# One first-layer matmul per step, issued in two, three or four column pieces

## The chip, the cores and the metric

The kernel runs on one core of a Trainium2 chip. The metric is the device time of one launch in microseconds; lower is better. A profile of one execution gives, beside that time, the span from the first to the last instruction of the program and every instruction's start and length.

## What is computed

Two stages follow one another. The first is a spectral mixer on `x` of shape (8, 3008, 256); the second a two-layer network on its 24064 rows.

```python
X = rfft(x, axis=1)                       # 8 batches, length 3008 along the rows
Yr = Xr @ w_r - Xi @ w_i + b_r
Yi = Xr @ w_i + Xi @ w_r + b_i
Y  = sign(Y) * max(abs(Y) - 0.01, 0)      # real and imaginary part
y  = irfft(Y, n=3008, axis=1)
h  = y.reshape(24064, 256) @ w_in         # 256 -> 2048
g  = where(h > 0, h, exp(min(h, 0)) - 1)
out = g @ w_out                           # 2048 -> 256
```

## The kernel before, in words

**The main loop (L1050).** The network is cut into 47 blocks of 512 rows, and each block into 8 pairs of 128 of the 2048 hidden columns: 376 steps, one pair of one block each. A step has a first layer and a second layer.

- First layer: `front_mm(i, h, 0)` and `front_mm(i, h, 1)` (L836, matmuls at L841). Each fills one tile `hps` of 128 hidden columns by 512 rows with two bf16 matmuls, `dt` 0 and 1, for the two halves of the 256 input columns. Where a block of 512 rows lies across the edge of two batches, `pieces` (L823) gives two stretches of rows, and each is a matmul of its own; that is so in 7 of the 47 blocks, so in 56 steps.
- The activation: ScalarE (L855, L856 or L858), GpSimd (L863) and VectorE (L875) turn `hps` into `gT`, in fp32r (a 4-byte form that TensorE takes).
- Second layer: `back(i - 2)` (L879, matmuls at L893), two steps behind: 8 matmuls, each with a 128 x 128 piece of `gT` as weights and 256 columns of `w_out_r` streamed, into `ps_o`. "The group" below is these 8.

**The units.** The mixer of the next batches is cut into units that run inside the steps, at most one per step, issued between `front_mm(i, h, 0)` and `front_mm(i, h, 1)`:

- A (L145): two fp32r matmuls of 512 columns;
- X (L188): eight bf16 matmuls of 96 columns;
- M (L250): six bf16 matmuls of 256 columns;
- B (L331): four bf16 matmuls of 256 columns (for batch 1, eight of half height);
- Y (L389): eight bf16 matmuls of 94 columns.

`units()` (L945) gives each unit its step ahead of time, from due times of the batches, and `plan()` (L1011) puts it into `f0[i]`. Of the 376 steps 84 have an M, 62 a Y, 56 an X, 42 a B, 36 an A and 96 have no unit. The order on TensorE is the order of issue:

```python
front_mm(i, h, 0)
for f, a in f0[i]:
    f(*a)                 # the unit, if there is one
front_mm(i, h, 1)
...
back(i - LAG)             # LAG = 2
```

Nothing reorders it. What TensorE can wait for is a free `hps` (4 buffers, two steps' worth, given back by L875), a `gT` that is ready (L875), and the data of the unit. Every matmul goes with a load of its 128 x 128 weights (the row PEld of the profile), also where the same weights are there already.

Of the kernel before, what the change touches and what calls it, by code (L numbers as in the profile page):

```python
# [25 lines left out]
def kernel(  # L26
# [11 lines left out]
    nc = tc.nc  # L38
    P = nc.NUM_PARTITIONS
# [20 lines left out]
    w_in_s = constp.tile([P, 2, DFF], BF16, name="w_in_s")  # L60
# [31 lines left out]
    TB = 512  # L92
# [17 lines left out]
    yT_of = {}  # L110
# [316 lines left out]
    with tc.tile_pool(name="stagep", bufs=1) as stagep:  # L427
# [3 lines left out]
        def col(eng, src, s1, op0, s2=None, op1=None, n=1, dt=F32):  # L431
            t = stagep.tile([P, n], dt, name=f"c{len(cols)}")
            cols.append(t)
            if op1 is None:
                eng.tensor_scalar(t[:], src[:], s1, None, op0)
            else:
                eng.tensor_scalar(t[:], src[:], s1, s2, op0, op1)
            return t

        def mix(eng, a, sc, b, op0, op1, n=1):  # L440
            t = stagep.tile([P, n], F32, name=f"c{len(cols)}")
            cols.append(t)
            eng.scalar_tensor_tensor(t[:], a[:], sc, b[:], op0, op1)
            return t
# [72 lines left out]
        c1 = mix(dve, qcol, -2.0, pcol, ALU.mult, ALU.add)  # L517
        c0 = col(dve, c1, -1.0, ALU.mult, 1.0, ALU.add)
# [304 lines left out]
    def pieces(t, k):  # L823

        out_, c = [], 0
        while c < k:
            b, r = divmod(t + c, S)
            e = min(k, c + S - r)
            out_.append((b, r, c, e))
            c = e  # L830
        return out_

    def front_ps():
        return [psH.tile([P, TB], F32, name="hps", tag="hps")[:] for _ in range(2)]

    def front_mm(i, hps, s):  # L836
        blk, fp = divmod(i, NPAIR)
        ft = 2 * fp + s
        for b, t0, c0, c1 in sorted(pieces(blk * TB, TB), key=lambda z: z[3] - z[2]):
            for dt in range(2):  # L840
                nc.tensor.matmul(  # L841
                    hps[s][:, c0:c1], lhsT=w_in_s[:, dt, ft * P : ft * P + P],
                    rhs=yT_of[b][:, dt, t0 : t0 + c1 - c0],
                    start=(dt == 0), stop=(dt == 1),
                )

    class Elu:
        def __init__(self, i, hps, mode):
# [162 lines left out]
    def plan():  # L1011

        f0 = [[] for _ in range(n + PER)]
        f1 = [[] for _ in range(n + PER)]
        mid = [[] for _ in range(n + PER)]
        at, xat = units()
        for (kind, b, k), t in at.items():
            if kind == "M" and k < 11 and (
                k % 2 == 0 if b == 1 else at[kind, b, k + 1] == t + 1
            ):  # L1020
                whole.add((b, k))
        for (kind, b, k), t in at.items():
            if t == 0:
                continue
            name = "Y" if kind == "y" else kind
            f0[t].append(put(name, b, *((k // 2, k % 2) if kind == "M" else (k,))))
            if (kind, k) == ("X", 7):
                for j in range(2):
                    mid[t + 1 + j].append((unit_D, (b, j)))
            if (kind, k) == ("B", 5):  # L1030
                f1[t + (b > 1)] += [(load_Bs, (b, w)) for w in range(4)]
            if (kind, k) == ("A", 5):
                for p in range(2 if b == 2 else 4):
                    w = 8 if p == 0 or b > 2 else 24
                    f1[t + (0, 1, 3)[min(max(b - 2, 0), 2)] * p].append((load_Z, (b, 8 * p, 8 * p + w)))
        for (b, c), t in xat.items():
            f1[t].append((load_x, (b, c)))
        for k in range(3):
            f1[5 + k].append((weight_sum, (k,)))
        for c in range(2):  # L1040
            f1[24 + c].append((turn_M3, (c,)))
            f1[4 + c].append((scale_w_in, (3, True, slice(FQ // 2 * c, FQ // 2 * c + FQ // 2))))
        return f0, f1, mid

    NST = 2
    f0, f1, mid = plan()
# [3 lines left out]
    for i in range(n + LAG):  # L1050
        split = False
        if i < n:
# [3 lines left out]
            h = front_ps()  # L1056
            e = Elu(i, h, "dve" if i < 4 else {"M": "act", "F": "pool"}[kind])
            front_mm(i, h, 0)
            for f, a in f0[i]:
                f(*a)  # L1060
            front_mm(i, h, 1)
            if was:
                was.mix(1 if kind == "M" and len(was.todo) == 2 else 0 if kind == "M" else 2)
# [69 lines left out]
```

## Time and profile before

| what | value |
|---|---|
| time, median of 3 runs | 884.24 us (883.89 to 884.44) |
| time of the profiled execution | 884.42 us |
| its span, first to last instruction | 882.4 us |
| granted TensorE clock, mean | 1.000 |
| TensorE matmul busy | 866.6 us, 6745 matmuls |
| second-layer matmuls (L893) | 3008 recorded, 478.9 us |
| first-layer matmuls (L841) | 1728 recorded, 438.3 us |
| ScalarE, VectorE, GpSimd busy | 726.7, 658.4 and 653.3 us |

The time of a run is some 2 us more than the span, which leaves out what lies around the program. A matmul's recorded length (382 ns for 512 columns at L841) is more than the distance from its start to the next one's, so successive matmuls overlap in the record: what one costs is that distance. The trace gives these starts to the nanosecond.

### The profile page before, as it was taken

To read this page: it belongs to the slowest core of one execution; us is meant where nothing else is said; L and a number is where in the kernel's file an instruction comes from. 1 tells how busy PE (TensorE), PEld (TensorE's weight loads), DVE (VectorE), ACT (ScalarE), POOL (GpSimd) and SP (SyncE) were. 2 spreads that over 40 slices of the span, in tenths; PEclk is the share of its full clock that TensorE was granted. 3 is DMA by queue.
4 is the path that set the end of the run, shared out by engine and by line. 5 is a ranking of instruction groups with operands and counts; after the bars stand their busy time and mean duration, and the time that the engine had idled before them with its cause. 6 is when DMAs were issued, how large, how long until landed. Compare 5 with 4: busy or idle time off the path is not lost.

```text
span 882.4 us, 18403 instructions
## 1 busy us (share of the span) xinstructions
PE 866.6 (98%) x6745; PEld 672.0 (76%) x6745; DVE 658.4 (75%) x1066; ACT 726.7 (82%) x1217; POOL 653.3 (74%) x981
## 2 busy tenths in 40 slices
PE   8889999999999999999999999999999999999997
PEld 3447777877788777878779777787777877787775
DVE  8767886688777787677876777767776688777775
ACT  6668998899878998899978999789987888786664
POOL 6707995689767887698866888668886699756664
PEclk9999999999999999999999999999999999999999
DMA  8994346743485443643464444553444023431111
GB/s 263 348 266 132 94 121 186 194 145 94 120 247 160 118 122 107 173 143 94 132 177 138 129 123 118 156 168 91 134 119 136 25 67 83 119 88 32 43 31 49
DMA packets 106374, 116.55 MB, mean 132 GB/s; under 512 B 10886, under 2 KB 96012, under 8 KB 103404
## 3 DMA queue, kind: packets, MB, share of 16 engines
q1 hardware_dynamic: 100124, 87.85, 35.8%
q0 software_dynamic: 6016, 27.40, 10.0%
q8 instruction: 53, 0.87, 0.4%
q14 instruction: 37, 0.30, 0.1%
q10 hardware_dynamic: 144, 0.13, 0.0%
HBM read 55.32 MB, written 49.81 MB: 119 GB/s over the span
## 4 chain that ended last, share of the span: by engine, by line
PE 86%; POOL 5%; DVE 5%; DMA 2%; issue 1%; ACT 1%; SPq 0%; POOLq 0%; DVEq 0%
PE ps_o L893 36%; PE hps L841 34%; PE mps L262 5%; PE xps L197 2%; PE aps L163 2%; PE yps L397 2%; POOL Et L863 2%; PE bps L356 1%; PE mps L214 1%; POOL Y L293 1%; DVE gT L875 1%; DMA w_in_f<-in_moe_w_in_dram 1%; PE bps L347 1%; DMA xt<-in_x_dram 1%; DVE yb L279 1%
## 5 line engine op out<-in xcount | busy, mean ns | idle before, releaser
L875 DVE SCALAR_TENSOR_TENSOR gT<-Et,hps 128x512 fp32r<-128x512 f32 x752 | 493.5, 684 | 161.6 <-POOL Et L863 160.3
L893 PE MATMUL ps_o<-w_out_r,gT 128*128 128x256 f32 x3008 | 478.9, 301 | 0.1
L863 POOL TENSOR_SCALAR Et<-Et 128x512 f32<-128x512 f32 x576 | 351.5, 618 | 166.5 <-ACT Et L858 165.3
L893 PEld LDWEIGHTS ps_o<-w_out_r,gT 128*128 128x128 f32 x3008 | 403.9, 188 | 49.7 <-DVE gT L875 0.3
L841 PE MATMUL hps<-yT,w_in_s 128*128 128x512 bf16 (+4 forms) x1728 | 438.3, 354 | 2.6 <-DVE gT L875 1.4
L858 ACT ACTIVATE Et<-hps 128x512 f32<-128x512 f32 x584 | 343.7, 605 | 99.5 <-PE hps L841 95.8
L841 PEld LDWEIGHTS <-w_in_s 128*128 128x128 bf16 x1728 | 121.6, 98 | 57.0 <-issue 16.6
L855 ACT ACTIVATE Et<-hps 128x512 f32<-128x512 f32 x168 | 99.6, 593 | 19.0 <-PE hps L841 17.9
L856 ACT ACTIVATE Et<-Et 128x512 f32<-128x512 f32 x168 | 106.4, 633 | 5.3
L293 POOL TENSOR_TENSOR Y<-yb,clip 128x512 bf16<-128x512 f32 x84 | 108.7, 1294 | 0.3
L288 POOL TENSOR_TENSOR yb<-yb,bias_d 128x256 f32<-128x256 f32 x68 | 49.8, 733 | 30.2 <-DVE yb L279 29.9
L289 POOL TENSOR_SCALAR clip<-yb 128x512 f32<-128x512 f32 x84 | 51.7, 616 | 13.5 <-DVE yb L275 5.8
L246 POOL TENSOR_TENSOR Xd<-XT 128x256 bf16<-128x256 bf16 x84 | 56.6, 674 | 0.0
L130 ACT CAST A<-aps 128x1024 bf16<-128x1024 f32 x45 | 45.3, 1009 | 7.2 <-PE aps L163 7.1
L130 ACT CAST XT<-xps 128x768 bf16<-128x768 f32 x61 | 48.5, 795 | 3.0 <-PE xps L197 3.0
L130 ACT CAST yT<-yps 128x752 bf16<-128x752 f32 x63 | 49.2, 782 | 2.0 <-PE yps L397 2.0
L262 PE MATMUL mps<-wsum,XT 128*128 128x256 bf16 x336 | 50.4, 273 | 0.0
L279 DVE TENSOR_TENSOR yb<-mps,Kb 128x512 f32<-128x512 f32 x68 | 47.1, 692 | 2.5
L278 DVE TENSOR_TENSOR Kb<-mps,bias_bc 128x256 f32<-128x256 f32 x68 | 28.7, 422 | 23.6 <-PE mps L262 23.6
L163 PE MATMUL aps<-xt,M 128*128 128x512 f32 x96 | 38.1, 478 | 2.5 <-DMA xt<-in_x_dram 2.1
L397 PEld LDWEIGHTS <-Bs 96*128 96x128 bf16 x512 | 28.3, 98 | 15.1 <-DMA Bs<-DB 1.8
L197 PEld LDWEIGHTS <-Z 96*128 96x128 bf16 x512 | 28.7, 97 | 13.3 <-issue 2.6
(124 smaller groups left out, 516.0 us busy)
## 6 DMA issues: line engine op xcount, KB each, us to landing
xt<-in_x_dram POOLq DMA_DIRECT2D x21, 1024.0 KB, 5.5
out_dram<-osb SPq DMA_DIRECT2D x158, 128.0 KB
Bs<-DB SPq DMA_DIRECT2D x32, 384.0 KB
DA<-A SPq DMA_DIRECT2D x21, 512.0 KB
DB<-Bz SPq DMA_DIRECT2D x20, 512.0 KB
Z<-DA SPq DMA_DIRECT2D x26, 384.0 KB
Yt<-Y SPq DMA_DIRECT2D x144, 64.0 KB
xt<-in_x_dram POOLq DMA_DIRECT2D x6, 512.0 KB, 6.2
```

Source lines behind the costliest of these rows:

```text
L130: nc.scalar.copy(dst, src)
L246: nc.gpsimd.tensor_tensor(Xd_of[b, k][:], XT[:, :, 0, o : o + P], XT[:, :, 1, o : o + P], ALU.subtract)
L262: nc.tensor.matmul(dst, lhsT=lhs(dt), rhs=rhs(dt), start=dt == 0, stop=dt == 1)
L279: nc.vector.tensor_tensor(two(yb[:]), two(ps[:, 0]), Kb.unsqueeze(1).to_broadcast([P, 2, D]), ALU.add)
L293: nc.gpsimd.tensor_tensor(Y_, two(yb), two(clips[0]), ALU.subtract)
L841: nc.tensor.matmul(hps[s][:, c0:c1], lhsT=w_in_s[:, dt, ft * P : ft * P + P], rhs=yT_of[b][:, dt, t0 : t0 + c1 - c0], start=(dt == 0), sto ...
L855: nc.scalar.activation(e, h, AF.Relu, scale=-1.0)
L856: nc.scalar.activation(e, e, AF.Exp, scale=-1.0)
L858: nc.scalar.activation(e, h, AF.Exp)
L863: nc.gpsimd.tensor_scalar(e, e, 1.0, 0.0, ALU.min, ALU.max)
L875: nc.vector.scalar_tensor_tensor(g_of[self.i][:, p], self.E[:, p], -1.0, self.h[p], ALU.add, ALU.max)
L893: nc.tensor.matmul(po[q][:, i_ % 2, :], lhsT=gT[:, s, i_ * P : i_ * P + P], rhs=w_out_r[:, ft, :], start=(ft == 0 and i_ % 2 == 0), stop=( ...
```

## The change

`front_mm` gets a table. In a block that lies in one batch, one of the step's four first-layer matmuls is issued in pieces of columns: with an M the second one (`s` 0, `dt` 1) in 2 pieces of 256, with a B the second one in 4 pieces of 128, without a unit the second one in pieces of 160, 160 and 192, with an A the third one (`s` 1, `dt` 0, the first after the unit) in 2 pieces of 256. Steps with an X or a Y, and those whose block lies across two batches, keep their matmuls. The pieces have the same weights, each loaded again, and write neighbouring columns of the same tile. Where the cut matmul is the first of its tile (A), only its first piece carries the start mark. The step number 0, which has no unit, is cut like the others without one.

Counted over the plan, 80 steps with M, 42 with B, 33 with A and 91 without a unit are cut: 80 + 3 x 42 + 33 + 2 x 91 = 421 more matmuls, and as many more weight loads. No other engine's instruction, no DMA and no wait is added, and the order stays as it is.

```diff
+    CUTS = {None: (0, 1, 3), unit_M: (0, 1, 2), unit_B: (0, 1, 4), unit_A: (1, 0, 2)}
+
     def front_mm(i, hps, s):
         blk, fp = divmod(i, NPAIR)
         ft = 2 * fp + s
-        for b, t0, c0, c1 in sorted(pieces(blk * TB, TB), key=lambda z: z[3] - z[2]):
+        parts = sorted(pieces(blk * TB, TB), key=lambda z: z[3] - z[2])
+        cs, cdt, ncut = CUTS.get(f0[i][0][0] if f0[i] else None, (0, 0, 1))
+        for b, t0, c0, c1 in parts:
             for dt in range(2):
-                nc.tensor.matmul(
-                    hps[s][:, c0:c1], lhsT=w_in_s[:, dt, ft * P : ft * P + P],
-                    rhs=yT_of[b][:, dt, t0 : t0 + c1 - c0],
-                    start=(dt == 0), stop=(dt == 1),
-                )
+                k = ncut if len(parts) == 1 and (s, dt) == (cs, cdt) else 1
+                edge = [c0 + (c1 - c0) * z // (32 * k) * 32 for z in range(k)] + [c1]
+                for a, z in zip(edge, edge[1:]):
+                    nc.tensor.matmul(
+                        hps[s][:, a:z], lhsT=w_in_s[:, dt, ft * P : ft * P + P],
+                        rhs=yT_of[b][:, dt, t0 + a - c0 : t0 + z - c0],
+                        start=(dt == 0 and a == c0), stop=(dt == 1), skip_group_check=ncut > 1 and len(parts) == 1 and s == cs,
+                    )
```

## The prediction

> **What bounds the kernel now.** I read the page first: busy shares, clock, chain.
>
> ```profile
> PE 866.6 (98%) x6745; PEld 672.0 (76%) x6745; DVE 658.4 (75%) x1066; ACT 726.7 (82%) x1217; POOL 653.3 (74%) x981
> PEclk9999999999999999999999999999999999999999
> PE 86%; POOL 5%; DVE 5%; DMA 2%; issue 1%; ACT 1%; SPq 0%; POOLq 0%; DVEq 0%
> ```
>
> TensorE is busy 98% of the span at full clock, and the chain that ended last is TensorE for 86%. Then the sums by stretch, to see whether that holds everywhere (columns: length, then busy time and count of PE, PEld, DVE, ACT, POOL).
>
> ```profile
> 200.00:300.00 100.00, 100.00 (x786) 79.99 (x784) 74.99 (x119) 88.26 (x148) 75.89 (x111) 1.00 0.51 148
> 700.00:760.00 60.00, 59.92 (x440) 46.78 (x439) 48.40 (x82) 52.72 (x91) 55.05 (x76) 1.00 0.26 71
> ```
>
> It does: from 60 us on TensorE never rests, and the nearest other engine is at 88 to 92%. So a matmul more is time on the path, and only what makes TensorE's own stream shorter can win. The timeline of TensorE shows that this stream has two speeds. First steps with an X, then a B, an M and a B:
>
> ```profile
> 77.70 1.26 PE L893 MATMUL ps_o<-w_out_r,gT 128*128 128x256 f32 x8
> 78.80 0.60 PE L841 MATMUL hps<-yT,w_in_s 128*128 128x512 bf16 x2
> 79.24 0.51 PE L197 MATMUL xps<-M,Z 96*128 96x96 bf16 x8
> 79.58 0.60 PE L841 MATMUL hps<-yT,w_in_s 128*128 128x512 bf16 x2
> 79.83 1.26 PE L893 MATMUL ps_o<-w_out_r,gT 128*128 128x256 f32 x8
> ```
>
> ```profile
> 401.75 1.29 PE L893 MATMUL ps_o<-w_out_r,gT 128*128 128x256 f32 x8
> ...
> 406.52 1.29 PE L893 MATMUL ps_o<-w_out_r,gT 128*128 128x256 f32 x8
> 407.65 0.60 PE L841 MATMUL hps<-yT,w_in_s 128*128 128x512 bf16 x2
> 408.10 0.60 PE L356 MATMUL bps<-Yt,M 128*128 128x256 bf16 x4
> 408.53 0.59 PE L841 MATMUL hps<-yT,w_in_s 128*128 128x512 bf16 x2
> 408.78 1.26 PE L893 MATMUL ps_o<-w_out_r,gT 128*128 128x256 f32 x8
> ```
>
> The same 8 second-layer matmuls take 1.26 or 1.29 us. By the starts in the trace the **short form** has a start every 113.33 ns, in 89 of 373 groups and to the same hundredth in each; the **long form** has 117.8 ns. From the group's second start to the next step it is 797 ns (median) against 826: a long group costs 29 ns more. In steps whose block lies in one batch, Y steps are short in 37 of 45, X in 22 of 27, B in 12 of 36 of the four-matmul kind, M in 0 of 80, A in 0 of 33, steps without a unit in 7 of 90 (six of them had waited for an `hps` just before). Some 284 groups are long.
>
> What decides is a rhythm of 6.667 ns: 113.33 is 17 of it. I tried periods between 1.7 and 100 ns for which the second starts of short groups fall together over the whole span and those of long ones do not; 6.667 and its half come out ahead of all others. Within it, the short groups' second starts all lie in one stretch of about 2 ns. Traced back to the moment at which the last first-layer matmul has streamed, X and Y steps get the short form if that moment falls in a window of about 1.7 ns, B steps if it falls in one of about 0.9 ns that lies 2.5 ns earlier in the rhythm; nearly everything outside is long. A step that begins with a short group and lasts a whole number of rhythms hands its place on. X lasts 2133.3 ns then (320 of them), Y 2126.7 (319): both whole, and these are the kinds that stay short. After a short group M lasts 2444.2 (366.6), B 2225.8 (333.9), A about 2271 (340.6), a step without a unit 1789.2 (268.4): none is whole.
>
> **The change, part by part.** What it adds is 421 matmuls. Their price comes from the first-layer shapes that are there already (the trace's groups by shape, mean length in ns last of the two):
>
> ```profile
> L841 PE MATMUL hps<-yT,w_in_s 128*128 128x512 bf16 x1280 | 371.1, 382 | 2.6 <-DVE gT L875 1.4 <-ACT yT L130 0.5
> L841 PE MATMUL hps<-yT,w_in_s 128*128 128x256 bf16 x64 | 9.7, 274 | 0.0
> L841 PE MATMUL hps<-yT,w_in_s 128*128 128x128 bf16 x64 | 9.0, 222 | 0.0
> L841 PE MATMUL hps<-yT,w_in_s 128*128 128x64 bf16 x64 | 7.3, 196 | 0.0
> ```
>
> Start to start, 512 columns take 215.8 ns, 256 take 109, 128 take 55.5, 64 take 28 to 29: 0.4167 ns a column and 2.5 ns per matmul. So a cut costs 2.5 ns per added piece: 2.5 for M and A, 5 without a unit, 7.5 for B, together 421 x 2.5 = **1.05 us**, all of it on the path. The 421 weight loads are recorded at 98 ns each, but pieces of 64 columns already start 28 ns apart, so the loads overlap and add nothing. The fp32r load ahead of the group (190 ns) still has a whole 512-column matmul (215.8 ns) to hide under, since the last first-layer matmul stays whole; behind a piece of 128 it would stick out by 134 ns. ScalarE gets `hps` later by 2.5 to 7.5 ns, and it rests 18% of the span.
>
> The Trainium skill, page "TensorE: Matmul & The Clock Gate", section "Back-to-back issue gap", speaks against the change: in a stream of loads and matmuls it gives some 81 ns per matmul at 128 columns. By it the four pieces of a B would last 324 ns, 108 more than the whole matmul, and the 42 cut B steps would cost 4.5 us instead of 0.3. The rows of this trace (55.5 ns at 128 columns) disagree, and I go by them.
>
> What it moves is the rhythm. After a short group the cut steps last: M 2446.7 ns, 367 rhythms exactly; B 2233.3, 335 exactly; A about 2273.5, 341 within what I can read; no unit 1794.2, 269 and 0.8 ns over. So M, B and A become steps that hand a short group on, and X and Y to M map the middle of one window to within 0.1 ns of the middle of the other. Steps without a unit drift by 0.8 ns each, most of a window's width.
>
> How many groups turn short the trace of before can't show: no M step there arrives in the middle of the window (the nearest, four arrivals at its lower edge, were long). Bounds: from nothing to all. Against all: entries from X and Y are spread over 1.7 ns, and M's window, if it is like B's, takes half of them; long groups shift the place by 0 to 5 ns, and about a quarter of the places (the 1 ns behind the window) give a long group that hands itself on just as exactly; the 56 uncut steps at batch edges have other lengths; A's own fp32r pair varies by 5 ns. Between the ends I take: M 50 of 80, B 12 more, A 10 of 33, no unit 3 more: 75 groups x 29.3 = 2.20 us. Net 2.20 - 1.05 = 1.15 us. Against the profiled execution's own 884.42 that is 883.3; the median of the runs lies 0.2 lower, so **883.1 us**.
>
> What is late next where TensorE gets faster: in 700 to 760 us GpSimd is busy 55.05 of 60, and five steps there already wait 164 ns each for an `hps`. About 20 steps in that stretch could give nothing back, at most 0.6 us, and that is inside my choice.
>
> **The rivals.**
> - *M, B and A lock, steps without a unit don't.* M 75, B 24 more, A 27: 126 x 29.3 = 3.69; less 1.05 gives 881.6. For: the whole numbers above. Against: narrow window.
> - *All lock,* steps without a unit too (73 more): 199 x 29.3 = 5.83, less 1.05: 879.5. Their window is unseen between 0.4 ns before its presumed middle and 1.5 ns behind it, so it may be wider.
> - *The cut does nothing for the rhythm.* M's 80 groups, all long, have some reason of their own, and the place of arrival isn't it: only the pieces remain, 884.24 + 1.05 = 885.3.
> - *Slower: short groups are lost.* If the new arrivals leave Y and X in the quarter of places that hands a long group on, the 59 short ones there go: 1.73 + 1.05 = 2.8, 887.0. It decides once more short groups are lost than M and B gain.
> - *Slower by loads.* If loads of equal weights can't overlap, a piece lasts 98 ns: B 392 instead of 216, 42 x 176 = 7.4; no unit 294, 91 x 78 = 7.1: 898.7. It decides below 98 ns per piece (229 columns); the 28 ns of 64-column pieces speak against it. By the 81 ns of the page named above it would be some 889.5.
>
> **The numbers.** Forecast (partial lock) 0.43; M, B and A lock 0.15; all lock 0.13; nothing 0.21; short groups lost 0.05; loads 0.03. The forecast's own spread is 881.8 to 884.5. The range 880.0 to 885.6 leaves out most of "all lock" and the two slow cases. Faster by over 0.2% (under 882.5, about what a measurement of this kernel can tell from no change): 0.15 + 0.13 + 0.07 of the forecast = 0.35; within it 0.36 + 0.21 = 0.57; slower 0.08.
>
> **What would show it.** In the profile after: groups of 1.26 us behind M and B in the timeline; M steps of 2446.7 ns from start to start; 256, 160 and 128-column pieces starting 109, 69 and 55.5 ns apart; 7166 matmuls. Wrong if cut M steps that follow a short group still have long ones, if pieces start 98 ns apart, or if TensorE starts to wait for `hps` or `gT` elsewhere.

## The result and the profile after

The changed kernel takes **882.44 us** (median of 22 runs, 881.5 to 885.47); the kernel before, run beside it, 883.9 (median of 22, 882.23 to 885.79). The ratio is 0.9986 with a 95% interval of 0.998 to 0.9993: 1.2 us less, between 0.6 and 1.8. The forecast was 1.15 less. In absolute time it was 883.1, and 882.44 was measured; the kernel before, too, came out 0.34 lower than the 884.24 that the forecast started from.

The page of the profiled execution of the changed kernel, the same rows as before:

```profile
span 882.7 us, 19139 instructions
...
PE 867.5 (98%) x7059; PEld 699.7 (79%) x7166; DVE 657.5 (74%) x1066; ACT 725.9 (82%) x1217; POOL 651.7 (74%) x981
...
PEclk9899999999999999999999999999999999999999
...
PE 85%; POOL 6%; DVE 5%; DMA 2%; issue 1%; ACT 1%; SPq 0%; POOLq 0%; DVEq 0%
```

The loads show the 7166 matmuls that were expected (107 matmul records are missing, so PE shows fewer). The span is no shorter than before's 882.4: this one execution took 1.3 us longer up to some 85 us, where nearly nothing is changed yet (its granted clock was 0.94 in the first 60 us, against 1.00 before). What the change did is therefore read from the main loop behind it. The sums by stretch (length, then busy time and count of PE, PEld, DVE, ACT, POOL; clock; DMA share; GB/s):

```profile
0.00:60.00 60.00, 53.01 (x298) 24.08 (x304) 43.20 (x89) 37.48 (x54) 32.77 (x63) 0.94 0.97 283
200.00:300.00 100.00, 99.95 (x822) 83.03 (x835) 74.92 (x119) 88.23 (x147) 76.66 (x113) 1.00 0.50 147
700.00:760.00 60.00, 59.70 (x471) 49.22 (x479) 48.45 (x81) 52.60 (x90) 55.07 (x76) 1.00 0.26 71
```

Two things are to be seen. From 200 us on the clock is 1.00 and TensorE nearly as full as before, so a comparison there is fair. And in 700 to 760 us its busy time is 59.70 where it was 59.92: some 0.2 us of new rest, which comes back below.

"The loop" in what follows is the time from the start of the step behind the eleventh group (near 85 us) to the start of the last step (near 873 us), as a difference of two starts in the trace. It is **787.61 us before and 786.66 after**: 0.95 less. In two more profiled executions of the changed kernel it is 786.55 and 786.71.

The timeline of TensorE. First the end of an M step before:

```profile
405.84 0.60 PE L262 MATMUL mps<-wsum,XT 128*128 128x256 bf16 x4
406.28 0.59 PE L841 MATMUL hps<-yT,w_in_s 128*128 128x512 bf16 x2
406.52 1.29 PE L893 MATMUL ps_o<-w_out_r,gT 128*128 128x256 f32 x8
```

And after, with an M, a B, an A and an M (some matmul records are missing: one at 399.65, for example):

```profile
399.00 0.38 PE L262 MATMUL mps<-wcat_r,Xd 128*128 128x256 bf16 x2
399.21 0.60 PE L262 MATMUL mps<-wsum,XT 128*128 128x256 bf16 x4
399.65 0.38 PE L848 MATMUL hps<-yT,w_in_s 128*128 128x512 bf16 x1
399.90 1.26 PE L900 MATMUL ps_o<-w_out_r,gT 128*128 128x256 f32 x8
401.00 0.61 PE L848 MATMUL hps<-yT,w_in_s 128*128 128x512 bf16 x5
401.45 0.60 PE L356 MATMUL bps<-Yt,M 128*128 128x256 bf16 x4
401.89 0.59 PE L848 MATMUL hps<-yT,w_in_s 128*128 128x512 bf16 x2
402.13 1.26 PE L900 MATMUL ps_o<-w_out_r,gT 128*128 128x256 f32 x8
...
404.40 1.26 PE L900 MATMUL ps_o<-w_out_r,gT 128*128 128x256 f32 x8
...
406.85 1.26 PE L900 MATMUL ps_o<-w_out_r,gT 128*128 128x256 f32 x8
```

The group behind an M, 1.29 us in all 80 such steps before, is 1.26 now, and so are those behind the B and the A. (L900 and L848 are the old L893 and L841.) The distances of the groups can be read off too: 402.13 - 399.90 = 2.23 us for the B step, 2.27 for the A step, 2.45 for the next M step. By the second starts, from one short group to the next, M steps take 2447 ns (median), and on average B steps 2233.4, A 2273.4, X 2133.3, Y 2126.5.

The plainest sign is what comes behind a short group. Before, all 24 M steps (with the block in one batch) that followed a short group had a long one, 22 of them after 2444 ns. After, 47 of 50 have a short one, and the other three took 43 to 134 ns more than 2447: they had waited.

The pieces by shape (mean length in ns last of the two numbers behind the bar):

```profile
L848 PE MATMUL hps<-yT,w_in_s 128*128 128x256 bf16 x290 | 53.2, 274 | 0.0
L848 PE MATMUL hps<-yT,w_in_s 128*128 128x160 bf16 x182 | 27.5, 233 | 0.1
L848 PE MATMUL hps<-yT,w_in_s 128*128 128x128 bf16 x232 | 25.3, 220 | 0.0
```

Recorded lengths are within 2 ns of those before (274 and 222), and next to nothing idles ahead of them. By their starts they follow each other at 109 ns (256 columns), 69 (160) and 55.8 (128).

Short groups counted from the starts (113.17 to 113.50 ns a start; before, all had 113.33):

| | before | after | after, 2nd | after, 3rd |
|---|---|---|---|---|
| M, of 80 cut | 0 | 58 | 60 | 56 |
| B, of 42 cut | 13 | 25 | 30 | 30 |
| A, of 33 cut | 0 | 15 | 15 | 14 |
| no unit, all | 7 | 2 | 1 | 1 |
| X, Y and the rest | 69 | 71 | 74 | 72 |
| all 373 | 89 | 171 | 180 | 173 |

So 82 groups more are short. From a group's second start to the moment at which the next step streams (the start of its second matmul, less the 213.3 ns of 512 columns at 0.4167) a short one takes 810.8 ns and a long one 839.3, 28.5 apart: 82 x 28.5 = 2.34 us. The pieces in this stretch cost 1.03. TensorE's waits inside the steps (gaps between starts beyond what the shapes take), most of them of the first layer for an `hps`, add up to 3.14 us before and 3.65 after: 0.5 more. 2.34 - 1.03 - 0.5 = 0.8 of the 0.95 measured; the 0.15 left is of the size by which the counted steps can be mis-sized and is not explained.

Such a wait, in the timeline of all engines (a step without a unit, behind an M step):

```profile
752.75 1.87 DVE L882 SCALAR_TENSOR_TENSOR gT<-Et,hps 128x512 fp32r<-128x512 f32 x3
752.81 0.63 ACT L863 ACTIVATE Et<-Et 128x512 f32<-128x512 f32 x1
752.83 0.47 PEld L848 LDWEIGHTS <-w_in_s 128*128 128x128 bf16 x5
752.83 1.24 PE L848 MATMUL hps<-yT,w_in_s 128*128 128x512 bf16 x6
...
753.49 0.10 PEld L848 LDWEIGHTS <-w_in_s 128*128 128x128 bf16 x1 [0.19 <-issue]
753.72 1.29 PE L900 MATMUL ps_o<-w_out_r,gT 128*128 128x256 f32 x8
```

PEld idles 0.19 us ahead of the load of the last first-layer matmul, and the step's six matmuls last 1.24 us from first start to last end, 0.2 more than six in a step without a wait (1.04, in the timeline of experiment 6). VectorE, which frees the `hps` (L882), works without a break just then: the `hps` comes no earlier when TensorE does. The matmul that waits, the first into the step's second `hps`, starts 51 to 54 ns after the end of an L882 (L875 before), in the trace of before as in this one. The five steps of this kind at 716 to 753 us waited 179 to 181 ns each before and some 204 now: 24 more, which is the 28.5 that the short group ahead saves, less 5 for the step's own two pieces. Together that is 0.13 of the 0.5 us. Most of the rest lies between 210 and 660 us, likewise in steps behind an M; one of these, a Y step at 427 us, had not waited before.

### The profile page after: what moved, and what is told of

Read it like the earlier page. It is cut to its first block, busy times and chain, and to the rows that moved or that the text cites. A ratio compares the mean times of both kernels' runs of the same rounds, so it can differ in the third digit from the quotient of the medians.

```text
span 882.7 us, 19139 instructions
## 1 busy us (share of the span) xinstructions
PE 867.5 (98%) x7059; PEld 699.7 (79%) x7166; DVE 657.5 (74%) x1066; ACT 725.9 (82%) x1217; POOL 651.7 (74%) x981
## 4 chain that ended last, share of the span: by engine, by line
PE 85%; POOL 6%; DVE 5%; DMA 2%; issue 1%; ACT 1%; SPq 0%; POOLq 0%; DVEq 0%
PE ps_o L900 37%; PE hps L848 32%; PE mps L262 5%; PE xps L197 3%; PE aps L163 2%; POOL Et L870 2%; PE yps L397 2%; PE bps L356 1%; POOL Y L293 1%; PE mps L214 1%; DVE gT L882 1%; DMA w_in_f<-in_moe_w_in_dram 1%; DVE yb L279 1%; POOL yb L288 1%; PE bps L347 1%
## 5 line engine op out<-in xcount | busy, mean ns | idle before, releaser
L882 DVE SCALAR_TENSOR_TENSOR gT<-Et,hps 128x512 fp32r<-128x512 f32 x752 | 493.5, 684 | 161.9 <-POOL Et L870 160.4
L900 PE MATMUL ps_o<-w_out_r,gT 128*128 128x256 f32 x3008 | 476.5, 301 | 0.1
L900 PEld LDWEIGHTS ps_o<-w_out_r,gT 128*128 128x128 f32 x3008 | 402.2, 188 | 46.0 <-DVE gT L882 0.3
L848 PE MATMUL hps<-yT,w_in_s 128*128 128x512 bf16 (+6 forms) x2047 | 417.6, 314 | 2.8 <-DVE gT L882 1.4
L848 PEld LDWEIGHTS <-w_in_s 128*128 128x128 bf16 x2149 | 152.8, 98 | 60.4 <-issue 15.6
```

The costliest lines, as they stand in the source:

```text
L848: nc.tensor.matmul(hps[s][:, a:z], lhsT=w_in_s[:, dt, ft * P : ft * P + P], rhs=yT_of[b][:, dt, t0 + a - c0 : t0 + z - c0], start=(dt == 0 ...
L882: nc.vector.scalar_tensor_tensor(g_of[self.i][:, p], self.E[:, p], -1.0, self.h[p], ALU.add, ALU.max)
L900: nc.tensor.matmul(po[q][:, i_ % 2, :], lhsT=gT[:, s, i_ * P : i_ * P + P], rhs=w_out_r[:, ft, :], start=(ft == 0 and i_ % 2 == 0), stop=( ...
```

## The experiments

**The theory (rhythm).** Whether a group is short is decided by where in a 6.667 ns rhythm the step reaches it; the added pieces act by lengthening the step by some ns, to a whole number of rhythms. **Rivals:** the *piece theory*: a first-layer matmul made in pieces, as such, lets the group behind it start in its short form, wherever it arrives; and the *load theory*: pieces cost more than 2.5 ns, through their weight loads, or what they give comes from how loads and matmuls overlap. Each kernel is an edit of the changed one. All were run beside the kernel before; times are medians. Experiments 1, 2, 4 and 5 ran on one chip, 3 and 6 on a second, 7 and 8 on a third, so times of different experiments are compared by their ratio to the kernel before, and by the loop.

**1. Other lengths.** If the rhythm rules, the same cuts with one piece more or less must lose the gain.

```diff
-    CUTS = {None: (0, 1, 3), unit_M: (0, 1, 2), unit_B: (0, 1, 4), unit_A: (1, 0, 2)}
+    CUTS = {unit_M: (0, 1, 3), unit_B: (0, 1, 3), unit_A: (1, 0, 3)}
```

> M, B and A steps are cut in three pieces each instead of two, four and two; steps without a unit are whole. 310 matmuls more than the kernel before. Rhythm theory: a step after a short group now lasts 2449.2 ns with M (367.4 rhythms), 2230.8 with B (334.6), some 2276 with A (341.4): none is whole, so M has at most 15 short groups of 80, A at most 5, B at most 14 of 42, and the pieces' 310 x 2.5 = 0.78 us come back nearly bare: ratio to the kernel before 1.0003 to 1.0010. Piece theory: as good as the changed kernel, ratio 0.9986 or less, M short in 50 or more.

Measured: 884.79 us (883.9 to 888.46), ratio 1.0012 (0.9998 to 1.0026); loop 788.75, 1.14 us longer than before. Short: M 1, B 0, A 0, 78 in all. Its timeline, two groups behind cut steps:

```profile
399.84 0.60 PE L848 MATMUL hps<-yT,w_in_s 128*128 128x512 bf16 x2
400.09 1.29 PE L900 MATMUL ps_o<-w_out_r,gT 128*128 128x256 f32 x8
...
402.35 1.29 PE L900 MATMUL ps_o<-w_out_r,gT 128*128 128x256 f32 x8
```

M and A steps have more pieces than in the change (three instead of two) and long groups; B, with three instead of four, lost even the 13 that it had. The piece theory falls. The loop fits 11 groups lost and 0.78 us of pieces: 0.31 + 0.78 = 1.1.

**2. The same length from elsewhere.** The first layer of M steps is left whole, and one of the unit's own six matmuls is cut in two, which also adds 2.5 ns (in all 84 M steps, the four at batch edges too).

```diff
-    CUTS = {None: (0, 1, 3), unit_M: (0, 1, 2), unit_B: (0, 1, 4), unit_A: (1, 0, 2)}
+    CUTS = {None: (0, 1, 3), unit_B: (0, 1, 4), unit_A: (1, 0, 2)}
...
-                nc.tensor.matmul(dst, lhsT=lhs(dt), rhs=rhs(dt), start=dt == 0, stop=dt == 1)
+                h = D // 2 if dt and dst is kp else D
+                for o_ in range(0, D, h):
+                    nc.tensor.matmul(
+                        dst[:, o_ : o_ + h], lhsT=lhs(dt), rhs=rhs(dt)[:, o_ : o_ + h],
+                        start=dt == 0, stop=dt == 1, skip_group_check=dst is kp,
+                    )
```

> As the changed kernel, but in steps with M the first layer is whole and one of the unit's own matmuls (256 columns) is issued in two pieces of 128: the same 2.5 ns at another place. Rhythm theory: only the step's length counts, M short in 50 to 65 of 80 and the time of the changed kernel, ratio 0.9982 to 0.9990. Piece theory (the first layer's cut itself helps): M short in 0 to 10, the time 1.5 to 2 us above the changed kernel, ratio 1.0003 to 1.0010.

Measured: 882.98 us (882.02 to 884.9), ratio 0.9994 (0.9985 to 1.0002); loop 786.71. Short: M 62 of 80, B 28, A 16, 184 in all; the ratio lies above the range that was expected, the count in it. An M step and the group behind it (L853 is the first layer, L905 the second):

```profile
398.51 0.38 PE L264 MATMUL mps<-wcat_r,Xd 128*128 128x256 bf16 x3
398.73 0.60 PE L264 MATMUL mps<-wsum,XT 128*128 128x256 bf16 x4
399.17 0.59 PE L853 MATMUL hps<-yT,w_in_s 128*128 128x512 bf16 x2
399.41 1.26 PE L905 MATMUL ps_o<-w_out_r,gT 128*128 128x256 f32 x8
```

There are three matmuls at the first row where the changed kernel has two, the first layer is whole, and the group is short. Between these two matmuls, what matters is the length and not which of them gives it; experiment 8 has one for which that does not hold.

**3. Three rhythms further.** M's three matmuls ahead of the last one get 3 added pieces each, nine in all: 22.5 ns, so 20 ns or three rhythms more than the change's one piece. From here on a table gives the pieces of each of the step's matmuls:

```diff
-    CUTS = {None: (0, 1, 3), unit_M: (0, 1, 2), unit_B: (0, 1, 4), unit_A: (1, 0, 2)}
+    CUTS = {
+        unit_M: {(0, 0): 4, (0, 1): 4, (1, 0): 4}, unit_B: {(0, 1): 4}, unit_A: {(1, 0): 2},
+    }
...
-        cs, cdt, ncut = CUTS.get(f0[i][0][0] if f0[i] else None, (0, 0, 1))
+        cut = CUTS.get(f0[i][0][0] if f0[i] else None, {}) if len(parts) == 1 else {}
...
-                k = ncut if len(parts) == 1 and (s, dt) == (cs, cdt) else 1
+                k = cut.get((s, dt), 1)
```

> As e1_no_unit_uncut (no cut without a unit), but the M step has nine added pieces instead of one (first-layer matmuls one, two and three in four pieces each): 2466.7 ns after a short group, 370 rhythms, three more than with one piece. Rhythm theory: the same place, so M short in 50 to 65 of 80 all the same, and the time 80 x 8 x 2.5 = 1.6 us above e1_no_unit_uncut: ratio to the kernel before 1.0005 to 1.0015. If the number of pieces or their width sets the form: M short in under 20. If a piece costs more than 2.5 ns: more than 1.6 us above.

Measured: 884.21 us (882.7 to 886.3), ratio 1.0004 (0.9995 to 1.0014); loop 787.65. Short: M 55, B 29, A 15, 172 in all. An M step in its timeline (L850 first layer, L902 second):

```profile
399.92 0.62 PE L850 MATMUL hps<-yT,w_in_s 128*128 128x128 bf16 x8
400.38 0.38 PE L262 MATMUL mps<-wcat_r,Xd 128*128 128x256 bf16 x2
400.60 0.60 PE L262 MATMUL mps<-wsum,XT 128*128 128x256 bf16 x4
401.03 0.60 PE L850 MATMUL hps<-yT,w_in_s 128*128 128x128 bf16 x5
401.29 1.26 PE L902 MATMUL ps_o<-w_out_r,gT 128*128 128x256 f32 x8
```

The step is 20 ns longer and still gets its short group, so the place repeats after 20 ns; one piece beside it (experiment 1, 2.5 ns) does not. The whole gain is then eaten: 83 groups more than before x 28.5 = 2.37 against some 2.2 of pieces and 0.16 of more waits, where the loop shows 0.04 more than before.

**4. Is the cut of the steps without a unit worth its pieces?** Only the entry for them is taken out.

```diff
-    CUTS = {None: (0, 1, 3), unit_M: (0, 1, 2), unit_B: (0, 1, 4), unit_A: (1, 0, 2)}
+    CUTS = {unit_M: (0, 1, 2), unit_B: (0, 1, 4), unit_A: (1, 0, 2)}
```

> The cuts in steps with M, B and A stay, steps without a unit are issued whole again (182 matmuls less than the changed kernel). Rhythm theory (a group of second-layer matmuls is short if the step before it hands its place in the 6.667 ns rhythm on, so a step's length decides): the three-piece cut of 1794.2 ns steps leaves a drift of 0.8 ns and locks nothing, so the number of short groups stays as in the changed kernel (M 50 to 65 of 80, A 12 to 20, B 22 to 28, without a unit 4 to 9), and the time falls by the pieces' 182 x 2.5 = 0.46 us: ratio to the kernel before 0.9981. Piece theory (any cut of a first-layer matmul speeds what follows): it loses up to 0.5 us, ratio 0.9990 or more.

Measured: 882.59 us (881.6 to 885.0), ratio 0.9992 (0.9983 to 1.0001); loop 786.73. Short: M 58, B 33, A 15, no unit 1, 176 in all. M and A are as expected; B is above its range (22 to 28) and no unit below it (4 to 9). The sum is that of the changed kernel (171 to 180), so those pieces bring no short group. The time missed: 0.9981 was expected, and 0.9992 is on the piece theory's side, though nothing in the counts is. The 0.46 us that the pieces cost does not show in the loop either, because TensorE's waits are 4.10 us in this execution, against 3.65 to 3.71 in the changed kernel. The difference is one wait of 436 ns by the starts, and it is not for an `hps`: at 256 us an X unit waits for a transfer (the 0.27 us in the brackets begin where the matmul before has ended in the record).

```profile
256.21 0.51 PE L197 MATMUL xps<-M,Z 96*128 96x96 bf16 x8 [0.27 <-DMA Z<-DA]
```

The half-height kernel of experiment 6 has no cut without a unit either, and not this wait: its loop is 786.24, 0.3 to 0.5 us below the three of the changed kernel. So by the loop the cut of the steps without a unit costs about what its pieces cost; by time the kernels can't be told apart.

**5. A whole number for the steps without a unit.** Seven added pieces make the step 1806.7 ns, 271 rhythms (the same edit of `front_mm` as in experiment 3):

```diff
+        None: {(0, 0): 3, (0, 1): 4, (1, 0): 3}, unit_M: {(0, 1): 2}, unit_B: {(0, 1): 4},
+        unit_A: {(1, 0): 2},
```

> As the changed kernel, but steps without a unit have seven added pieces (first-layer matmuls one, two and three in 3, 4 and 3 pieces, the fourth whole): 1806.7 ns after a short group, 271.0 rhythms. Rhythm theory: these steps now hand their place on, 30 to 80 of the 91 get a short group (the changed kernel: 1), the other kinds keep theirs; 91 x 5 x 2.5 = 1.14 us more pieces against 0.9 to 2.3 us: ratio to the kernel before 0.9973 to 0.9989. If steps without a unit have no window of their own: still under 10 short, ratio 0.9999.

Measured: 882.78 us (881.9 to 884.34), ratio 0.9991 (0.9982 to 0.9999); loop 786.53. Short: no unit 34 (33 of them cut, one in a block at a batch edge), M 54, B 29, A 15, 205 in all; the ratio is a little above the range expected (0.9973 to 0.9989). A step without a unit that begins with a short group ends with one, 1806.7 ns on, in 32 of 37 cases. But the last 40 or so, which follow each other with nothing between, are all long (L903 second layer):

```profile
837.64 1.29 PE L903 MATMUL ps_o<-w_out_r,gT 128*128 128x256 f32 x8
838.77 1.05 PE L851 MATMUL hps<-yT,w_in_s 128*128 128x160 bf16 x11
839.47 1.29 PE L903 MATMUL ps_o<-w_out_r,gT 128*128 128x256 f32 x8
```

Their second starts follow each other at 1833.35 ns on average, which is 275.00 rhythms, so they lie at one and the same place, some 0.8 ns behind the window: long groups, too, hand their place on there.

**6. Alternating.** Steps without a unit get 4 and 2 added pieces in turn, to move the place to and fro across the window; the half-height B of batch 1 gets 2 pieces instead of 4. The second edit was also made alone (key "b"; the keys 0 and 1 are steps without a unit by turns):

```diff
+        unit_M: {(0, 1): 2}, unit_B: {(0, 1): 4}, "b": {(0, 1): 2}, unit_A: {(1, 0): 2},
+        0: {(0, 1): 3, (1, 0): 3}, 1: {(0, 1): 3},
```

> As e7_half_height_b, and steps without a unit get four and two added pieces by turns: after a short group 1799.2 ns (0.8 ns short of 270 rhythms) and 1794.2 (0.8 ns over 269), so two of them together hand the place on for 7.5 ns a step instead of 17.5. Rhythm theory: 40 to 85 of the 91 short, for one of the two places lies in the window and often both; 91 x 7.5 = 0.68 us of pieces against 1.2 to 2.5 us: ratio to the kernel before 0.9962 to 0.9982, the best of all. If a drift of 0.8 ns is always too much: under 20 short, ratio as e7_half_height_b or 0.0008 above.

> As e1_no_unit_uncut, but the six B steps of batch 1 (eight matmuls of half height) have their matmul in two pieces, not four: after a short group some 2440 ns, 366 rhythms, where four pieces give 366.75. Rhythm theory: 4 or 5 of these 6 turn short (2 in the changed kernel) and hand the place on to the M steps between them, M 60 to 70 of 80; 0.3 to 0.5 us less than e1_no_unit_uncut, ratio 0.9978 to 0.9990. Otherwise: as e1_no_unit_uncut.

Both missed their counts. Alternating: 881.56 us (880.27 to 885.16), ratio 0.9986 (0.9975 to 0.9997), loop 786.17; no unit 32 instead of 40 to 85, and the ratio above its range (0.9962 to 0.9982). The place goes to and fro, but one of the two positions is outside: in the last blocks exactly every other group is short.

```profile
836.23 1.26 PE L912 MATMUL ps_o<-w_out_r,gT 128*128 128x256 f32 x8
837.33 1.04 PE L860 MATMUL hps<-yT,w_in_s 128*128 128x512 bf16 x6
838.02 1.29 PE L912 MATMUL ps_o<-w_out_r,gT 128*128 128x256 f32 x8
839.15 1.05 PE L860 MATMUL hps<-yT,w_in_s 128*128 128x512 bf16 x8
839.85 1.26 PE L912 MATMUL ps_o<-w_out_r,gT 128*128 128x256 f32 x8
```

So the window of these steps is no wider than the drift of some 0.8 ns. Half-height B alone: 882.12 us (880.81 to 883.67), ratio 0.9988 (0.9979 to 0.9997), loop 786.24; none of the 6 is short, where 4 or 5 were expected (2 are in the changed kernel). Which place these steps need was not found.

**7. A nudge.** Experiment 5 with one edit more: in the one step number 336 (42 x 8, without a unit) four pieces are added instead of seven, which moves all behind it by -7.5 ns, one rhythm and 0.8 ns.

```diff
+        unit_A: {(1, 0): 2}, 42 * NPAIR: {(0, 1): 3, (1, 0): 3},
```

> As e3_no_unit_whole, where 33 of the steps without a unit became short and the 40 of the last blocks stayed long, at one place some 0.8 ns behind that of the short ones, each handing that place on. Here one step, the first without a unit after the last batch edge (block 42), has four added pieces instead of seven: 0.8 ns less in the rhythm, once. Rhythm theory: that one nudge turns the 39 steps behind it short, 65 to 78 of the 90; against the changed kernel 91 x 5 x 2.5 = 1.1 us more pieces and 65 to 78 x 29.3 = 1.9 to 2.3 us of groups, so some 1.0 us less: ratio to the kernel before 0.9970 to 0.9982. If long runs there have another reason: 33 short as in e3_no_unit_whole, ratio 0.9988 to 0.9995.

Measured: **881.85 us** (880.3 to 884.58), ratio 0.9978 (0.9965 to 0.9991); loop 785.25, which is 2.36 less than before and 1.46 less than the changed kernel run again beside it (786.71). Short: no unit 77 instead of 34, 254 in all. The same stretch as in experiment 5:

```profile
838.03 1.26 PE L903 MATMUL ps_o<-w_out_r,gT 128*128 128x256 f32 x8
839.13 1.05 PE L851 MATMUL hps<-yT,w_in_s 128*128 128x160 bf16 x11
839.84 1.26 PE L903 MATMUL ps_o<-w_out_r,gT 128*128 128x256 f32 x8
```

The steps are the same eleven matmuls, and all 39 behind the nudge are short. A place a fraction of a ns off, and nothing else, had made them long. By ratio and loop this is the best version found. Its median is 0.93 us below that of the changed kernel beside it (882.78), but the intervals of the two ratios overlap; that it is faster than the changed kernel rests on the medians and on the loop.

**8. The load ahead of the group.** Instead of its second first-layer matmul, an M step has its fourth one cut, the one just ahead of the group. The prediction had a cost for this: the 190 ns fp32r load would stick out from behind a short piece. No cut without a unit.

```diff
-    CUTS = {None: (0, 1, 3), unit_M: (0, 1, 2), unit_B: (0, 1, 4), unit_A: (1, 0, 2)}
+    CUTS = {unit_M: {(1, 1): 2}, unit_B: {(0, 1): 4}, unit_A: {(1, 0): 2}}
```

> As e1_no_unit_uncut, but in M steps it is the fourth first-layer matmul, the one just ahead of the second-layer group, that is in two pieces of 256 columns. The group's first weight load is recorded at 190 ns and begins with the matmul before it, which now lasts 109 ns instead of 215.8. If the load must end before the group begins, TensorE stands still for up to 81 ns in each of the 80 M steps and every M group starts elsewhere in the rhythm: 1 to 6.5 us above e1_no_unit_uncut, ratio to the kernel before 1.0000 to 1.0065, M short in few or many as the new length falls. If the load hides anyway: as e1_no_unit_uncut, ratio 0.9981 to 0.9992, M short in 50 to 65.

Measured: 884.07 us (883.22 to 884.82), ratio 1.0007 (0.9998 to 1.0015); loop 788.59. Short: M 0 of 80, B 13, A 6, 85 in all. Starts in one of its M steps, relative to the group's first recorded start:

```
 -29 ns  last piece, 256 columns
 -27 ns  first fp32r load of the group, 190 ns long
 +83 ns  second fp32r load, 192 ns long
+204 ns  second matmul of the group
+321 ns  third
```

From the last piece to the group's second matmul are 204 + 29 = 233 ns, where a piece of 109 and a long second-layer matmul of 117.8 make 227 without any stall. So some 6 ns were lost (5 in the median of the 80 steps), not the 81 by which 190 exceeds 109; and the second load starts while the first is still recorded as running. The time does lie in the range that was expected if the load must end first, but not for that reason: 80 stops of 81 ns would be 6.5 us, and the loop is 0.98 longer than before, which fits 239 pieces (0.60), 80 times 5 ns (0.40) and 4 groups lost (0.11), less 0.2 of shorter waits. The load theory has no support here either.

But no M step was short, though the step was lengthened by the same piece. The trace shows that it is not for arriving elsewhere: in 64 of the 80 M steps the last piece starts within 1 ns of the middle of those places in the rhythm at which the last matmul starts ahead of the short groups of the B and A steps (and 215.8 - 109 = 106.8 ns is 16 rhythms, so the end falls alike). From the same place these groups go long. So what stands directly ahead of the group also decides; whether it does so through those 5 ns is not shown.

**9. The changed kernel again**, twice, as a measure of how much the counts and the loop vary.

> The changed kernel once more, beside the next three on the same chip. Rhythm theory: the same places, so the same counts within a few groups (M 58 of 80, B 25 of 42, A 15 of 33, without a unit 2 of 96 short), ratio to the kernel before 0.9980 to 0.9993. If the counts were luck of one execution: M anywhere from 0 to 80.

> The changed kernel beside e9_whole_and_nudge on the same chip: ratio to the kernel before 0.9983 to 0.9992, M short in 55 to 62 of 80, without a unit 0 to 3.

Measured: 882.08 us (881.39 to 883.62), ratio 0.9988 (0.9979 to 0.9996), and 882.78 us (881.58 to 884.11), ratio 0.9991 (0.9983 to 1.0). Loops 786.55 and 786.71, short groups 180 and 173: together with the first profile the loop repeats within 0.16 us and the counts within 9; B is 30 in both, above the first profile's 25. The ratios of experiments 1 and 3 lie 0.0002 above and 0.0001 below the ranges that were expected, well inside their intervals.

## Why the prediction was right

It forecast 1.15 us less by short groups behind cut steps, and 1.2 less came in that way. The mechanism was the one forecast. That the size came so near is in part luck: the number of groups was a choice between nothing and all, and what came out better (M, A) stood against what came out worse (steps without a unit, waits). Step by step:

- **Price of a piece: right.** 2.5 ns each; pieces start 109, 69 and 55.8 ns apart, as read from the rows of before.
- **Loads overlap: right.** Loads are recorded at 98 ns and pieces of 128 columns start 55.8 apart, so a B step's four pieces take 223 ns. The Trainium skill, page "TensorE: Matmul & The Clock Gate", section "Back-to-back issue gap", has some 81 ns per matmul at 128 columns, 324 for the four; the trace does not agree here, and that rival is out.
- **Rhythm and whole numbers: right.** M steps of 2447 ns (2446.7 forecast), B 2233.4 (2233.3), A 2273.4 (2273.5) hand the short group on; experiments 1, 2, 3 and 7 show by loss, substitute, repeat and nudge that the place decides, and experiment 8 that what stands just ahead of the group does too. The forecast's own test, M steps behind a short group, came out short in 47 of 50. The prediction left half of 6.667 ns open. The 13 traces decide it: of the steps whose last first-layer matmul starts half a rhythm (to within 1 ns) from the middle of the short ones of their kind, all 163 have long groups (kinds with ten short groups or more in a trace).
- **Counts: right in sum.** M 58 (50 forecast), B 12 more (12), A 15 (10): these gave more than forecast. The steps without a unit went from 7 to 2 where 3 more were forecast: their 0.8 ns of drift is, by experiment 6, about the whole window, and of the seven short ones before, six had followed a wait (the seventh lies in a block across two batches, so the prediction's "7 of 90" is 6 of 90). 82 groups in all, 75 forecast; 28.5 ns each, 29.3 forecast.
- **"A long group that hands itself on": right,** and more costly than thought: 40 steps in experiment 5 sat in it until the nudge.
- **Waits for `hps`: near in size, wrong in place.** 0.5 of the "at most 0.6 us", but only some 0.15 of it in 700 to 760 us, where the forecast put it all; the rest lies in steps behind an M between 210 and 660 us. So one of its signs of being wrong, "if TensorE starts to wait for `hps` or `gT` elsewhere", did show, in small: 72 ns in the Y step at 427 us. The 164 ns that it gives for the waits of before are 180 by the starts, and "from 60 us on TensorE never rests" is too strong (before, it rests 1.5 us between 60 and 100 us). The forecast did not subtract the new waits: the loop lost 0.95 us, 0.2 less than the 1.15 forecast, and these 0.5, less the 0.14 by which the groups gave more (2.34 against 2.20), are more than that difference.
- **"Behind a piece of 128 it would stick out by 134 ns": wrong as a way of reckoning.** Behind a piece of 256 the same reckoning gives 81, and experiment 8 shows 5 to 6. Recorded length of a load is not time that the next matmul waits. It took no part in the sum, since the last matmul stayed whole. A piece of 128 there was not tried.

Open: what in the chip makes the two forms and the rhythm; why half of the A steps, 20 or so M steps and the half-height B stay long (19 of the 22 long M steps and 13 of the 18 long A steps follow a long group, but what place that one hands on was not traced); by what the piece just ahead of the group changes the form in experiment 8; and whether leaving out the cut without a unit is faster in the time as it is in the loop (experiments 4 and 6).

## What to carry to other kernels

When the same instructions appear in a trace with two lengths and nothing between, sort them by what ran before and by where they start, before taking the mean: here a mean of 116.7 ns (89 groups at 113.33, 284 at 117.8) hid 28 ns a step. A small delay at the right spot can be worth more than it costs, but it must be sized for each kind of step, and any wait or edge step upsets it, so the gain stays small (0.1% here, 0.2% with the nudge). When the bounding engine gets faster, look at the steps in which it already waited for another engine, over the whole span: there some of the gain comes back as waiting (0.5 of 2.3 us here).

## What the runs showed of the hardware

- Eight fp32r matmuls of 256 columns start every 113.33 ns or every 117.8 ns, and which of the two is settled for the whole group by a difference in arrival of less than 1 ns. The place repeats after 20 ns (experiment 3) and, by the lengths of the steps that hand it on (2133.3, 2126.5, 2447, 2233.4 and 1806.7 ns, whole multiples to within 0.4 ns), after 6.667 ns.
- A recorded weight load of 190 ns ahead of the group held up the next matmul by some 5 to 6 ns when only 109 ns of matmul stood in front of it, and the group was long then, wherever it arrived (80 of 80).
- A matmul cut into pieces of columns, each with its weights loaded again, costs 2.5 ns per added piece down to 128 columns (starts 109, 69 and 55.8 ns apart for 256, 160 and 128 columns).
